# A free PSUM bank for the fill work, and attention values stored by chunks of 512 keys

## The chip, the core and the metric

The kernel runs on one core of a Trainium2 chip. The metric is the device time of one execution in microseconds (us). Five engines work side by side: PE (TensorE, matrix products), ACT (ScalarE), DVE (VectorE), POOL (GpSimd) and SP (SyncE, which here issues every DMA). They wait for each other on semaphores; each engine works its own list of instructions strictly in order.

## The reference

Two independent parts are computed from two inputs of 2048 tokens by 448 features, and their results stand side by side in the output.

```python
# part A: Fourier mixing, real part
a = einsum("bsd,ed->bse", x, dft_hid_re)
b = einsum("bsd,ed->bse", x, dft_hid_im)
y = einsum("ts,bse->bte", dft_seq_re, a) - einsum("ts,bse->bte", dft_seq_im, b)

# part B: full attention, 16 heads of 28
q, k, v = split(x @ wqkv)
p = softmax(einsum("bhqd,bhkd->bhqk", q, k) * 28 ** -0.5)
o = einsum("bhqk,bhkd->bhqd", p, v)
out_B = concat_heads(o) @ wo
```

## The kernel before

Each matrix operand is split into a high and a low part, and a product is the sum of several products of such parts.

**Attention.** A projection product (`project`, run through the helper `chain`, L571) makes queries and keys, transposed, in tiles of 128 rows by 512 tokens; the two parts go through SP to the DRAM tensor `qk_d` and come back per head as `q` and `k` tiles. `values` makes V token tile by token tile (16 tiles of 128 tokens, eleven products each). For each head, `head_once` walks over 16 key tiles times four chunks of 512 queries. `score` (L1130) multiplies one key tile with one query chunk into a PSUM bank, and ACT takes the exponential of that bank into a half of a `kept` buffer (L1134). After sixteen scores, `four` (L1141) multiplies the sixteen exponentials with V: this is called a **block** below, 64 blocks in all, four to a head. A block is one task on PE: it is not interrupted, and it waits until all of its sixteen exponentials are done. Its output is the bank `po`, held for the whole head. A column of ones beside the values of each head gives the sum of the exponentials; the rest of the 32 columns that a head takes are zeros. `tops` finds a bound for each query row out of the first 32 keys (the "key products", L1114); the `qb` tile that it loads has one buffer.

**The fill.** Everything else that PE does stands between the scores: the remaining projections, the hidden transform of part A (`hidden_both`, L571), the sequence transform with its halved matrices (`combine` prepares its operands on ACT and DVE, `sequence_halved` multiplies, L901; `middle`, L849), and the output projection (`project_late`, L1364 and L1395). ACT also splits the loaded weights (L542, L890), copies projections out of their banks (L612), shares the plain copies with DVE (L436 is ACT's, L438 DVE's), and splits the attention output for the last projection (L1349).

**The order.** The order of instructions on every engine is written by a planner at build time, `Schedule`. It walks through a model of the engines with a guessed duration for every task, and each time that an engine is free it takes the task with the smallest key that is ready and whose buffers can be had. The keys are due times: scores of head h get keys spread evenly from `T_ATT` to `T_END`, the fill (`fkey`) keys up to `T_FILL`, the end of the output projection keys from `T_OUT`. SP's DMAs are planned the same way, so a DMA that has to wait holds back all DMAs behind it.

**The banks.** PSUM has eight banks. Four belong to `fill_s` and four to `bank_s`, which serves scores, key products and block outputs. `bank_s` may borrow from `fill_s` (its `lender`): in `can_take`, L117, the free banks of both are added up. The `kept` pool has 19 buffers, each a pair of 128 by 512 tiles.

**The values.** For each token tile, `values` takes one `kept` pair and uses its first half: DVE copies the 448 columns out of the bank into runs of 28 (L639), sets the ones (L640) and the zeros (L641), and SP stores the tile to `v_d` (L643), whose rows hold, per head and partition, 16 token tiles of 32 numbers. One store thus writes 2,048 runs of 128 bytes. `head_loads` (L1010) loads a head's values once all sixteen stores have landed.

Of the kernel before, what the change touches and what calls it, by code (L numbers as in the profile page):

```python
# [21 lines left out]
D = 448  # L22
H = 16
DH = 28
# [5 lines left out]
VW = 32  # L30
# [5 lines left out]
NQS = 8  # L36
NQB = 1
NFILL = 4
NQ = 4
QT = NT // NQ  # L40
Q_YO = 2
# [57 lines left out]
class Slots:  # L99
# [17 lines left out]
    def can_take(self, slots, before):  # L117
        n = sum(since <= before for _, since in self.free)
        if self.lender:
            n += sum(since <= before for _, since in self.lender.free)  # L120
        if n < len(slots) + max(s.spare for s in slots):
            return False
        if self.in_turn:
            return all(s in self.turns[:n] for s in slots)
        return True
# [187 lines left out]
def tile_kernel(ctx, tc, xa, wre, wim, wd, xb, wqkv, wo, out):  # L313
    nc = tc.nc
# [15 lines left out]
    v_d = dram.tile([H, P, NT * VW], F32, name="vd")  # L330
# [6 lines left out]
    mid_d = dram.tile([1, D], F32, name="midd")  # L337
    far_d = [dram.tile([P, D], F32, name=f"fard{n}") for n in range(2 * NQ)]

# [13 lines left out]
    kept_s = new("kept", [P, 2, CH], F32, NPAIRS)  # L353
# [9 lines left out]
    ones = new("ones", [P, 1])  # L363
    diff = new("diff", [P, 2 * NQ + 1, 3 * QT + 1])
    whole = new("whole", [P, 2 * NQ + 1])
    alike = new("alike", [P, 2, 2 * NQ + 1])
    edge = new("edge", [P, 4, NT])
# [12 lines left out]
    sch.pools.append(raw_s)  # L380
    fill_s, bank_s = Slots(banks[:NFILL]), Slots(banks[NFILL:])
    bank_s.lender = fill_s
# [5 lines left out]
    nc.gpsimd.memset(diff[:, :, 3 * QT:], 0.0)  # L388
    nc.gpsimd.memset(diff[:, 2 * NQ, 4:3 * QT], 0.0)
    nc.vector.tensor_tensor(fold, ident[:, :VW], ident[:, VW:2 * VW], op=ALU.add)  # L390
# [19 lines left out]
    M512, M448, MS = 0.2335, 0.2050, 0.2365  # L410
# [3 lines left out]
    def pe(key, emit, n=1, d=MS, lat=0.25, **kw):  # L414
        return sch.add({"PE": n * d}, key, emit, lat=lat, **kw)

    def dma(key, emit, size=256, extra=0.0, n=1, **kw):

        return sch.add({"SP": 0.4}, key, lambda e: emit(), dmas=[(size, extra)] * n, **kw)
# [4 lines left out]
    def dve(key, emit, d=DVE_P, **kw):  # L424
        return sch.add({"DVE": d}, key, lambda e: emit(), **kw)

    def pool(key, emit, d, **kw):
        return sch.add({"POOL": d}, key, lambda e: emit(), **kw)
# [9 lines left out]
            nc.vector.tensor_copy(dst, src)  # L438


    T_ATT, T_END, T_FILL, T_OUT = 34.0, 755.0, 824.0, 766.0
    units = [(h, c) for h in range(H - 1) for c in range(NC)] + [(H - 1, c) for c in LAST]
    due, head_due, head_due_b = {}, {}, {}

# [120 lines left out]
    def chain(key, seq, o, cols, deps, use, d, then=(), parts=None, last=last):  # L565


        n = len(seq)
        for i, (w, x) in enumerate(seq):
            def emit(e, i=i, w=w, x=x):  # L570
                nc.tensor.matmul(o.t[:, :cols], w(), x(), start=(i == 0), stop=(i == n - 1))  # L571
            more = [*(deps if i == 0 else ()), *(parts.get(i, ()) if parts else ())]
            last[0] = pe(key + i * d, emit, d=d, deps=[last[0], *more], use=[*use, o, *(then if i == n - 1 else ())])
        return last[0]

    def lz(f, *a):
        return lambda: f(*a)
# [3 lines left out]
    v_done = {}  # L581
# [40 lines left out]
        return Piece(lambda: wqkv[:, :, j * P:(j + 1) * P], 0.2 if j == 0 else key, "w", j == 0)  # L622

    def values(ready, chunks):
        for c in chunks:
            v_done[c] = []
            for t in range(4):
                tok = slice(c * CH + t * P, c * CH + (t + 1) * P)
                o, pair = fill_s.slot(), kept_s.slot()
                vs = Half(pair, 0)  # L630
                seq = products(lambda k: lz(x_h, k, tok), lambda k: lz(x_l, k, tok), lambda: lz(x_3, tok),
                               lambda k: (lambda: w_first.h[:, k]), lambda k: (lambda: w_first.l[:, k]))
                key = fkey(11, M448)
                end = chain(key, seq, o, D, [], [], M448, [pair],
                            {3 * k: [xb_ready[c, k], ready[k], *ready[4:][:k // 3]] for k in range(4)}, v_last)

                def put(o=o, vs=vs):
                    v3 = vs.t.rearrange("p (h d) -> p h d", h=H)
                    nc.vector.tensor_copy(v3[:, :, :DH], o.t[:, :D].rearrange("p (h d) -> p h d", h=H))  # L639
                    nc.vector.memset(v3[:, :, DH:DH + 1], 1.0)  # L640
                    nc.vector.memset(v3[:, :, DH + 1:], 0.0)  # L641
                b = dve(key - 20, put, 0.85, deps=[end], use=[o, pair])
                v_done[c].append(dma(key - 20, lambda vs=vs, c=c, t=t: nc.sync.dma_start(  # L643
                    v_d[:, :, (4 * c + t) * VW:(4 * c + t + 1) * VW].rearrange("h p x -> p h x"),
                    vs.t.rearrange("p (h x) -> p h x", h=H)), extra=2.5, deps=[b], use=[pair]))


    y_stored = {}
# [374 lines left out]
    before = {}  # L1023
# [202 lines left out]
    o = bank_s.slot()  # L1226
# [18 lines left out]
    key = fkey(0, 0)  # L1245
# [175 lines left out]
    o = bank_s.slot()  # L1421
# [64 lines left out]
```

## Time and profile before

| | us |
|---|---|
| median of three timed runs | 865.23 (864.64 to 870.12) |
| profiled execution | 868.95 |
| its span, first to last instruction | 866.7 |
| mean granted clock of PE | 0.98 |
| PE, ACT, DVE, POOL busy | 843.5, 634.9, 375.6, 6.0 |
| first block starts | 83.4 |
| last block starts | 827.6 |

In the page's costliest groups a row names line, engine, operation, output and input tiles, shape and count; then busy us and the mean ns of one; then the idle time of the engine before them and what ended it. The chain of waits is followed back from the last instruction and lists start, length and what the time was spent on. In the tables by stretches each engine's busy time stands for a stretch of the span, then PE's granted clock, the share of DMA time and GB/s.

### The profile page before, as it was taken

What the parts mean: (1) busy time and instruction counts of PE and PEld (TensorE: products, weight loads), DVE (VectorE), ACT (ScalarE), POOL (GpSimd) and SP (SyncE); (2) the same over time, 40 slices, a digit from 0 to 9 for tenths busy, and PEclk for the clock granted to TensorE, in tenths of its full rate; (3) what the DMA queues carried; (4) which work ended last, traced back from release to release, by engine and by line L of the source; (5) the groups of instructions that cost most, each with busy time, mean ns of one, the idle gap of its engine ahead of it and who ended that gap; (6) DMA issues with size and microseconds to landing.
All of it is one profiled execution on the core that took longest, in us unless ns stands there. A gap on an engine that the chain in (4) does not pass through costs nothing.

```text
span 866.7 us, 14119 instructions
## 1 busy us (share of the span) xinstructions
PE 843.5 (97%) x4856; PEld 532.5 (61%) x4856; DVE 375.6 (43%) x888; ACT 634.9 (73%) x1287; POOL 6.0 (1%) x27
## 2 busy tenths in 40 slices
PE   8988999999999999999999999999999999999896
PEld 7875455556555556666556655667566656666575
DVE  7541013111311132222379463667766575756341
ACT  6107787787877878878899766789887876788831
POOL 2000000000000000000000000000000000000000
PEclk9998999999999999999989999999899999999999
DMA  9867634424343454434597664558886653746433
GB/s 285 207 113 192 193 116 123 158 90 133 100 152 111 127 155 122 132 112 142 172 219 220 204 189 137 179 171 246 192 250 208 191 171 119 224 144 175 125 117 106
DMA packets 156239, 141.27 MB, mean 163 GB/s; under 512 B 69310, under 2 KB 125120, under 8 KB 156160
## 3 DMA queue, kind: packets, MB, share of 16 engines
q1 hardware_dynamic: 156160, 140.29, 54.9%
q8 instruction: 40, 0.66, 0.3%
q14 instruction: 39, 0.32, 0.1%
HBM read 98.82 MB, written 43.12 MB: 164 GB/s over the span
## 4 chain that ended last, share of the span: by engine, by line
PE 86%; ACT 5%; DMA 4%; DVE 2%; SPq 1%; issue 1%; ACTq 0%; DVEq 0%
PE bank L1130 27%; PE bank L1141 25%; PE bank L571 18%; PE bank L901 10%; ACT kept L1134 3%; PE bank L1364 3%; DMA wraw<-wre 1%; PE bank L849 1%; DMA kept<-ond 1%; DMA qb<-qkd 1%; PE bank L1114 1%; DMA kept<-xb 1%; PE bank L1395 1%; DMA v<-vd 1%; PE bank L1221 1%
## 5 line engine op out<-in xcount | busy, mean ns | idle before, releaser
L1134 ACT ACTIVATE kept<-bank 128x512 f32<-128x512 f32 x1024 | 522.9, 669 | 104.6 <-PE bank L1130 103.6
L1130 PE MATMUL bank<-q,k 85*128 85x512 f32 x1024 | 345.4, 416 | 7.2 <-ACT kept L1134 3.7
L1130 PEld LDWEIGHTS bank<-q,k 85*128 85x128 f32 x1024 | 184.2, 190 | 104.9 <-ACT kept L1134 50.5
L1141 PE MATMUL bank<-kept,v 128*32 128x512 f32 x2048 | 236.3, 602 | 0.9 <-DMA v<-vd 0.9
L1141 PEld LDWEIGHTS bank<-kept,v 128*32 128x32 f32 x2048 | 60.6, 111 | 136.1 <-issue 131.4
L901 PE MATMUL bank<-big,wlo 128*128 128x226 f32 x512 | 96.9, 285 | 0.0
L901 PEld LDWEIGHTS bank<-big,wlo 128*128 128x128 f32 x512 | 85.7, 202 | 15.1 <-issue 7.5
L571 PE MATMUL bank<-big,whi 128*128 128x512 f32 (+1 forms) x260 | 93.3, 397 | 1.3 <-DVE big L432 1.0
L901 PE MATMUL bank<-big,whi 128*128 128x448 f32 (+1 forms) x256 | 74.7, 338 | 0.2 <-ACT kept L1134 0.2
L873 DVE TENSOR_REDUCE diff<-wlo 128x1 f32<-128x512 f32 x96 | 65.6, 683 | 2.5
L571 PEld LDWEIGHTS bank<-big,whi 128*128 128x128 f32 x260 | 48.5, 190 | 16.3 <-issue 2.8
L901 PEld LDWEIGHTS bank<-big,whi 128*128 128x128 f32 x256 | 50.9, 208 | 7.6 <-ACT kept L1134 2.2
L891 DVE TENSOR_TENSOR wlo<-wraw,whi 128x512 fp32r<-128x512 f32 x32 | 22.0, 688 | 62.9 <-PE bank L901 49.5
L613 DVE TENSOR_TENSOR wd<-bank,wd 128x512 fp32r<-128x512 f32 x16 | 11.1, 691 | 82.9 <-ACT wd L612 82.9
L571 PE MATMUL bank<-big,wlo 128*128 128x512 f32 x112 | 44.6, 400 | 0.0
L571 PE MATMUL bank<-wd,whi 128*128 128x450 f32 (+1 forms) x128 | 43.0, 376 | 0.0
L438 DVE COPY kept<-bank 128x450 f32<-128x450 f32 (+2 forms) x31 | 19.3, 622 | 54.4 <-PE bank L571 54.0
L546 DVE TENSOR_TENSOR wlo<-wraw,whi 128x384 fp32r<-128x384 f32 x23 | 12.8, 556 | 69.2 <-ACT whi L542 60.7
L612 ACT ACTIVATE wd<-bank 128x512 fp32r<-128x512 f32 x16 | 10.8, 676 | 42.2 <-PE bank L571 42.2
L571 PE MATMUL bank<-wd,big 128*128 128x448 f32 x176 | 38.3, 376 | 0.0
L571 PEld LDWEIGHTS bank<-wd,big 128*128 128x128 f32 x176 | 33.9, 194 | 3.9 <-issue 0.9
L1364 PE MATMUL bank<-big 128*128 128x448 f32 x144 | 33.0, 368 | 0.0
(117 smaller groups left out, 588.6 us busy)
## 6 DMA issues: line engine op xcount, KB each, us to landing
wdraw<-wre SPq DMA_DIRECT2D x48, 256.0 KB
wdraw<-wim SPq DMA_DIRECT2D x48, 256.0 KB
qkd<-wd SPq DMA_DIRECT2D x32, 256.0 KB
q<-qkd SPq DMA_DIRECT2D x64, 112.0 KB
k<-qkd SPq DMA_DIRECT2D x64, 112.0 KB
abd<-kept SPq DMA_DIRECT2D x16, 448.0 KB
kept<-abd SPq DMA_DIRECT2D x16, 448.0 KB
qkd<-kept SPq DMA_DIRECT2D x24, 256.0 KB
```

The source lines that it names most:

```text
L438: nc.vector.tensor_copy(dst, src)
L546: b = dve(at, lambda: nc.vector.tensor_tensor(self.lo.t[:, :n], raw.t[:, :n], f32(self.hi.t)[:, :n], op=ALU.subtract), 0.15 * n, deps=[a], ...
L571: nc.tensor.matmul(o.t[:, :cols], w(), x(), start=(i == 0), stop=(i == n - 1))
L612: a = act(key, lambda o=o, hi=hi: nc.scalar.activation(as_r(hi.t), o.t, AF.Copy), deps=[end], use=[o, *own])
L613: b = dve(key, lambda o=o, hi=hi, lo=lo: nc.vector.tensor_tensor(as_r(lo.t), o.t, as_f(hi.t), op=ALU.subtract), deps=[a], use=[o, *own])
L873: seen.append(dve(key, lambda: nc.vector.tensor_reduce(dst, f32(flat(src.t)), axis=AX.X, op=ALU.max, apply_absolute_value=True), 0.6, deps ...
L891: b = dve_on(key - 11.5, lambda e: e.tensor_tensor(turned(lo.t), read(same.t), f32(turned(hi.t)), op=ALU.subtract), 0.65, deps=[a], acq=[l ...
L901: nc.tensor.matmul(o.t[:, at0:at0 + n], cut_of(w.t, e, c), x(), start=first, stop=stop)
L1130: m = pe(key, lambda e: nc.tensor.matmul(b.t, KT[h][kt // 4].t[:KR + 1, kt % 4 * P:(kt % 4 + 1) * P], q.t[:KR + 1, :], start=True, stop=True),
L1134: return act(key - 20, lambda: nc.scalar.activation(p.t, b.t, AF.Exp, scale=SCALE), deps=[m], use=[b, pair])
L1141: nc.tensor.matmul(o.t[j * VW:(j + 1) * VW, :], VT[h].t[:, kt // 4, kt % 4, :], tiles[i // 2].t[:, i % 2, :], start=(kt < 4 // len(cs)), s ...
L1364: nc.tensor.matmul(o.t[:, :D], a(), b(), start=(i == 0), stop=(i == 8 and n < N_HELD))
```

## The change

Three things are changed.

1. In `can_take`, scores (and all that draws on `bank_s`) may borrow all of the fill's free banks but one (`LEFT = 1`).
2. The planner's four due times move: attention from 28 to 723 instead of 34 to 755, the fill to 850 instead of 824, the last projection from 801 instead of 766.
3. `values` works on a chunk of 512 keys at a time. Two `kept` pairs hold the chunk, one for each eight heads, laid out so that the four token tiles of a head lie side by side. For each token tile DVE copies 8 heads into each pair, two copies instead of one. The ones and zeros of a pair are set once by POOL, in four memsets, with a key that lets them run early. SP then stores a pair with 1,024 runs of 512 bytes. There are eight stores instead of sixteen, and 32 memsets on POOL instead of 32 on DVE.

```diff
+LEFT = 1
...
         if self.lender:
-            n += sum(since <= before for _, since in self.lender.free)
+            n += max(0, sum(since <= before for _, since in self.lender.free) - LEFT)
...
-    T_ATT, T_END, T_FILL, T_OUT = 34.0, 755.0, 824.0, 766.0
+    T_ATT, T_END, T_FILL, T_OUT = 28.0, 723.0, 850.0, 801.0
...
     def values(ready, chunks):
+        HH = H // 2
         for c in chunks:
-            v_done[c] = []
+            v_done[c], puts = [], [[], []]
+            pairs = [kept_s.slot() for _ in range(2)]
+            heads = lambda pair: pair.t.rearrange("p a (b t x) -> p (a b) t x", t=4, x=VW)
             for t in range(4):
                 tok = slice(c * CH + t * P, c * CH + (t + 1) * P)
-                o, pair = fill_s.slot(), kept_s.slot()
-                vs = Half(pair, 0)
+                o = fill_s.slot()
...
-                end = chain(key, seq, o, D, [], [], M448, [pair],
+                end = chain(key, seq, o, D, [], [], M448, pairs,
...
-                def put(o=o, vs=vs):
-                    v3 = vs.t.rearrange("p (h d) -> p h d", h=H)
-                    nc.vector.tensor_copy(v3[:, :, :DH], o.t[:, :D].rearrange("p (h d) -> p h d", h=H))
-                    nc.vector.memset(v3[:, :, DH:DH + 1], 1.0)
-                    nc.vector.memset(v3[:, :, DH + 1:], 0.0)
-                b = dve(key - 20, put, 0.85, deps=[end], use=[o, pair])
-                v_done[c].append(dma(key - 20, lambda vs=vs, c=c, t=t: nc.sync.dma_start(
-                    v_d[:, :, (4 * c + t) * VW:(4 * c + t + 1) * VW].rearrange("h p x -> p h x"),
-                    vs.t.rearrange("p (h x) -> p h x", h=H)), extra=2.5, deps=[b], use=[pair]))
+                for i, pair in enumerate(pairs):
+                    if t == 0:
+                        def rest(pair=pair):
+                            blocks = pair.t.rearrange("p a (b x) -> p a b x", x=VW)
+                            for a in range(2):
+                                nc.gpsimd.memset(blocks[:, a, :, DH:DH + 1], 1.0)
+                                nc.gpsimd.memset(blocks[:, a, :, DH + 1:], 0.0)
+                        puts[i].append(pool(key - 25, rest, 1.2, use=[pair]))
+                    puts[i].append(dve(key - 20, lambda o=o, i=i, pair=pair, t=t: nc.vector.tensor_copy(
+                        heads(pair)[:, :, t, :DH], o.t[:, i * HH * DH:(i + 1) * HH * DH].rearrange("p (h d) -> p h d", h=HH)), 0.35,
+                        deps=[end], use=[o, pair]))
+            for i, pair in enumerate(pairs):
+                v_done[c].append(dma(key - 20, lambda i=i, pair=pair, c=c: nc.sync.dma_start(
+                    v_d[i * HH:(i + 1) * HH, :, 4 * c * VW:4 * (c + 1) * VW].rearrange("h p x -> p h x"),
+                    pair.t.rearrange("p a (b x) -> p (a b) x", x=4 * VW)), 512, extra=1.0, deps=puts[i], use=[pair]))
```

Bank numbers and due times reach the program only through the planner, so the order of the instructions shows what they do. The first place is PE's list around block 2, before the change: the last product of block 1, the scores (L1130) of the following blocks, the first product of block 2 (L1141). Banks 0 to 3 are the fill's.

```order
L1141 MATMUL bank1_271<-kept16_251,v0_223 32x512 x2
L1130 MATMUL bank5_275<-q1_226,k1_219 128x512
L1130 MATMUL bank6_276<-q2_227,k1_219 128x512
L1130 MATMUL bank7_277<-q3_228,k1_219 128x512
L1130 MATMUL bank4_274<-q0_225,k2_220 128x512
L1130 MATMUL bank2_272<-q1_226,k2_220 128x512
L1130 MATMUL bank5_275<-q2_227,k2_220 128x512
L1130 MATMUL bank3_273<-q3_228,k2_220 128x512
L1130 MATMUL bank6_276<-q0_225,k2_220 128x512
L1130 MATMUL bank0_270<-q1_226,k2_220 128x512
L1141 MATMUL bank1_271<-kept17_252,v0_223 32x512 x2
```

The same place after the change, up to the middle of what stands between blocks 1 and 2 (the lines are eight higher, L1138 the scores, L1149 the blocks, L572 the projections).

```order
L1149 MATMUL bank5_275<-kept1_236,v0_223 32x512 x2
L1138 MATMUL bank6_276<-q0_225,k1_219 128x512
L1138 MATMUL bank7_277<-q1_226,k1_219 128x512
L1138 MATMUL bank4_274<-q2_227,k1_219 128x512
L1138 MATMUL bank2_272<-q3_228,k1_219 128x512
L1138 MATMUL bank0_270<-q0_225,k1_219 128x512
L572 MATMUL bank1_271<-big_206,whi2_213 128x512
L1138 MATMUL bank6_276<-q1_226,k1_219 128x512
L572 MATMUL bank1_271<-big_206,wlo2_216 128x512
L1138 MATMUL bank7_277<-q2_227,k1_219 128x512
L572 MATMUL bank1_271<-big_206,whi2_213 128x512
L1138 MATMUL bank4_274<-q3_228,k1_219 128x512
```

Before, scores and the block output stand in all four of the fill's banks, and no fill stands between the blocks. Now a projection keeps a bank and advances by one product after nearly every score.

The second place is ACT's list near the end of the attention, before the change: L1349 splits the attention output, here the part that the second load brings; L1134 are exponentials, L436 is a copy.

```order
L1134 ACTIVATE kept_239<-bank_274 128x512
L1134 ACTIVATE kept_243<-bank_275 128x512
L1349 ACTIVATE big<-kept_248 128x512 x2
L1349 ACTIVATE big<-kept_237 128x512
L1349 ACTIVATE big<-kept_253 128x512
L1349 ACTIVATE big<-kept_237 128x512
L1349 ACTIVATE big<-kept_253 128x512
L436 ACTIVATE kept_241<-bank_277 128x512
L1134 ACTIVATE kept_243<-bank_276 128x512
L1134 ACTIVATE kept_244<-bank_274 128x512
```

The same place after (L1142 the exponentials, L1357 the splits, L1392 those of the last rows).

```order
L1142 ACTIVATE kept_237<-bank_271 128x512
L1142 ACTIVATE kept_243<-bank_277 128x512
L1142 ACTIVATE kept_243<-bank_275 128x512
L1357 ACTIVATE big<-kept_239 128x512
L1392 ACTIVATE q_225<-kept_252 128x512
L1357 ACTIVATE big<-kept_248 128x512 x2
L437 ACTIVATE kept_247<-bank_276 128x512
L1357 ACTIVATE big<-kept_246 128x512
L1357 ACTIVATE big<-kept_249 128x512
```

The six splits that follow the second load stood ahead of the last exponentials; now they stand behind them.

## The prediction

> **What bounds the kernel now.** I began with the page's busy times and costliest groups (busy us, mean ns of one, then idle before).
>
> ```profile
> PE 843.5 (97%) x4856; PEld 532.5 (61%) x4856; DVE 375.6 (43%) x888; ACT 634.9 (73%) x1287; POOL 6.0 (1%) x27
> ...
> L1134 ACT ACTIVATE kept<-bank 128x512 f32<-128x512 f32 x1024 | 522.9, 669 | 104.6 <-PE bank L1130 103.6
> L1130 PE MATMUL bank<-q,k 85*128 85x512 f32 x1024 | 345.4, 416 | 7.2 <-ACT kept L1134 3.7
> ```
>
> PE looks full, but its busy time is modelled: a matmul's mean here is 416 ns although scores follow each other far closer. So I counted by stretches of the span (PE, PEld, DVE, ACT, POOL busy; clock; DMA share; GB/s).
>
> ```profile
> 84.00:91.00 7.00, 7.00 (x39) 2.46 (x31) 0.69 (x1) 2.52 (x7) 0.00 (x0) 0.68 0.67 203
> 91.00:110.00 19.00, 19.00 (x100) 7.69 (x98) 0.75 (x2) 16.83 (x36) 0.00 (x0) 1.00 0.60 182
> 110.00:424.00 314.00, 313.87 (x1761) 185.86 (x1764) 70.24 (x141) 250.29 (x504) 0.61 (x2) 1.00 0.41 129
> ...
> 436.00:452.00 16.00, 15.96 (x77) 9.78 (x73) 11.64 (x32) 15.04 (x37) 0.00 (x0) 0.79 0.90 215
> ...
> 787.00:831.00 44.00, 41.77 (x239) 22.91 (x231) 19.25 (x39) 34.30 (x71) 0.00 (x0) 0.96 0.40 121
> ```
>
> From 110 to 424 ACT is idle for 64 us of 314. The waits of the stretch 91 to 424 (total, times, longest) say where, and the timeline of one block (start, length) says why.
>
> ```profile
> ACT kept L1134 <- PE bank L1130: 47.8, 45, 3.2
> ...
> PEld bank L1130 <- ACT kept L1134: 23.9, 103, 0.5
> ```
>
> ```profile
> 203.69 3.64 PE L1141 MATMUL bank<-kept,v 128*32 128x512 f32 x32
> ...
> 207.26 0.73 PE L571 MATMUL bank<-big,whi 128*128 128x512 f32 x2
> ...
> 208.76 0.40 PE L1130 MATMUL bank<-q,k 85*128 85x512 f32 x1
> ...
> 209.20 0.60 ACT L1134 ACTIVATE kept<-bank 128x512 f32<-128x512 f32 x1 [1.09 <-PE bank L1130]
> ```
>
> A block of sixteen PV products holds PE for 3.57 us (203.69 to 207.26). It starts only when its sixteen exponentials are done, and while it runs no score can follow, so ACT lives on the scores already standing in banks. It then runs dry until the next score plus a hand-over of 0.44 us (208.76 to 209.20). Between two such gaps ACT is nearly always busy. So the period of a block is set on ACT: 16 × 0.511 (522.9 / 1024) = 8.2 us of exponentials, plus whatever else ACT does, plus a dry time of 3.57 + 0.44 − 0.511 × (scores ahead). PE fills the rest with projection and Fourier products, and scores wait for ACT. The chain of waits confirms it at the start, where PE had no such products:
>
> ```profile
> 10.29 23.43 PE bank L571 x108
> ...
> 35.23 9.21 PE bank L571 x45
> ...
> 51.34 2.92 DMA qb<-qkd
> ...
> 78.08 5.14 DMA v<-vd
> 83.36 6.17 PE bank L1141 x32
> ...
> 91.86 3.57 PE bank L1141 x32
> ...
> 101.03 3.57 PE bank L1141 x32
> ...
> 110.20 3.57 PE bank L1141 x32
> ...
> 423.65 3.57 PE bank L1141 x32
> ...
> 707.41 3.80 DMA qb<-qkd
> ...
> 808.78 7.42 DMA kept<-ond
> ...
> 827.64 3.57 PE bank L1141 x32
> ...
> 846.77 10.88 PE bank L1364 x54
> ```
>
> Blocks 2 to 4 are 9.17 us apart with six scores ahead; the formula gives 8.2 + 4.0 − 3.1 = 9.1. Blocks 4 to 31 are 11.6 apart, blocks 31 to 64 about 12.2.
>
> **The change part by part.** The sum is made against the profiled execution, 868.95 us with a span of 866.7; it lies 0.4% above the median of the timed runs, 865.23, so I carry the difference over to the median.
>
> *Value stores.* Sixteen stores of 128-byte runs become eight of 512-byte runs. The DMA view of 45 to 50 us, nearly all value stores, and of 22 to 24 us, mostly 512-byte pieces of the weights, give the price (packets, MB, share of 16 engines):
>
> ```profile
> q1 hardware_dynamic: 5613, 0.71, 89.9%
> q1 hardware_dynamic: 615, 0.30, 69.0%
> ```
>
> The first is 0.899 × 16 × 5 / 5613 = 12.8 ns a packet, the second at most 36 ns. 32,768 packets at 12.8 ns over 16 engines are 26 us; 8,192 at 36 ns are 18 us, an upper bound. What counts for the end, though, is which wait goes with it:
>
> ```profile
> 42.80 5.32 SPq L643 DMA_DIRECT2D vd<-kept  x4
> L643 SPq DMA_DIRECT2D vd<-kept x16: 382/591/2790, 16.0 to 70.2; - x16
> ```
>
> Before the first PV block the chain waits 2.9 us for a load of qb, which stood in SP's queue behind four value stores, and 5.1 us for v, which needs all sixteen, the last issued at 70.2. In the new order the first block stands behind 111 projection, 176 value, 20 score and 4 key products. By rows, a value product is 9.21 / 45 = 0.205 us and a projection (23.43 − 64 × 0.205) / 44 = 0.235, a score of the same 512 columns likewise: 10.3 + 26.1 + 36.0 + 4.7 + 1.6 = 78.7 us, the key products at an estimated 0.4 each, under two scores' price. The last value store can be issued near 60 and the v load near 65, landing at 70: hidden with 8 us to spare. So block 1 starts at 78.7 instead of 83.4: **−4.7**. If the cover goes, nothing is gained there.
>
> *Edits I cost at nothing.* The new value copies (32 for 16, on DVE) and the memsets that leave DVE:
>
> ```profile
> 14.22 0.61 DVE L639 COPY kept<-bank 128x448 f32<-128x448 f32 x1
> 14.80 0.07 DVE L640 MEMSET kept<- 128x16 f32 x1
> 1.42 0.10 POOL L389 MEMSET diff<- 128x8 f32 x1
> 4.00 0.21 POOL L396 MEMSET kb<- 128x128 f32 x1
> ```
>
> A half copy lies between 0.31 and 0.61 us, so a token tile costs DVE 0.6 to 1.2 us while PE works 11 × 0.205 = 2.3 us on it. The 32 memsets on POOL are 3 to 7 us at 0.10 to 0.21; twelve of them now stand ahead of the zeros of the first projection weights, which thus come at 4.2 + 12 × 0.2 = 6.6, and PE starts at 10.3. The value buffers hold eight of nineteen kept pairs, so the last x loads wait for buffers in SP's queue; what they bring is first needed at 10.3 + 44 × 0.205 + 33 × 0.235 = 27 us, and the other eleven buffers turn over long before.
>
> *The bank left to the fill.* Four groups of ACT's other work set the prices of this part and the next:
>
> ```profile
> L612 ACT ACTIVATE kept<-bank 128x512 fp32r<-128x512 f32 x12 | 8.0, 670 | 3.7 <-PE bank L571 2.0 <-issue 1.3 <-PE bank L1130 0.4
> L436 ACT ACTIVATE kept<-bank 128x446 f32<-128x446 f32 (+3 forms) x23 | 13.4, 585 | 13.3 <-PE bank L1141 6.0 <-PE bank L1364 4.2 <-PE bank L571 3.0
> L542 ACT ACTIVATE whi<-wraw 128x512 fp32r<-128x512 f32 x23 | 16.8, 740 | 1.7 <-DMA wraw<-wqkv 1.7
> L1349 ACT ACTIVATE big<-kept 128x512 fp32r<-128x512 f32 x12 | 6.9, 627 | 2.3 <-DMA kept<-ond 2.3
> ```
>
> In the old order nothing but scores stands between blocks 1 and 4; now 12 to 14 projection products stand in each gap. These three periods become, with 3.7 scores ahead and 1.2 copies of a projection (L612) on ACT, 8.2 + 2.1 + 0.8 = 11.1 us instead of 8.9: **+6.5**. Block 4 then starts at 112.0, 1.8 us later than before, but with 62 more projection products and 3 fewer scores done: 13.9 us of PE work in hand. Whether that lead is worth anything depends on ACT.
>
> *What ACT is spared later.* Between blocks 5 and 64 the new order has 15 projection copies on ACT for 20, 8 copies of hidden and output rows for 20 (the others moved to DVE or past the end), 5 splits of the attention output for 12, one weight split fewer. 5 × 0.670 + 12 × 0.585 + 7 × 0.627 + 0.740 = 15.5 us by means; in a run they overlap as exponentials do (511 of 669), 11.8. I take **−14**.
>
> *Fewer scores ahead.* The price of the free bank: counted in the order, the scores ahead of a block fall from 4.15 to 3.56 (27 blocks) and from 3.12 to 2.56 (33 blocks), 0.30 and 0.29 us more dry time each. Against that, the fill between a block and its first score falls from 0.31 to 0.04 and from 0.20 to 0.02 us. Net 27 × 0.03 + 33 × 0.11 = **+4.4**.
>
> *The end.* 124 instead of 98 output products stand behind block 64: 26 × 10.88 / 54 = **+5.2**. In exchange the wait at 808.8 should go. It is ACT's: a split of the attention output (L1349) waits there for its load, and exponentials are queued behind it on ACT, scores behind these on PE, which from 787 to 831 is 2.2 us unbusy and loses 44 × 0.04 = 1.8 to the clock. In the new order the splits of that second load stand behind the last exponential: **−4**. The qb wait at 707 stays.
>
> Sum: −4.7 + 6.5 − 14 + 4.4 + 5.2 − 4 = −6.6 us: 862.3 for such an execution, **858.6** on the median's scale.
>
> **The rivals.**
> *PE sets the pace.* Then the 13.9 us in hand are kept, less the 1.8: 865.2 − 12.1 − 4 = 849. For it: scores wait only 23.9 us for ACT in 333. Against: ACT's gaps, which fit the formula. 0.25.
>
> *The start stays.* The v load stands behind stores of projections in SP's queue whatever the values do; if block 1 stays at 83.4 and the wait at the end finds a successor: 858.6 + 4.7 + 4 = 867, no change. 0.17.
>
> *ACT starves (slower).* Where the fill holds three banks and one stays free, scores have three. If the dry time grows by 0.30 a block but the fill ahead of the first score was hidden anyway (ACT still had work), 27 × 0.27 + 33 × 0.18 = 13.2 us are not won back; with ACT's lower price (2.2) and another wait at the end (4) that gives 878. It decides from a dry time of some 2.3 us a block on, against 47.8 / 28 = 1.7 now. 0.13.
>
> *The clock.* More short pauses on PE could halve its clock, as in 84 to 91 (0.68) and 436 to 452 (0.79). The loss is 7 × 0.32 = 2.2 and 16 × 0.21 = 3.4 us there; six such stretches more, at 2.8 on average, are +17: 876. The Trainium skill (TensorE: Matmul & The Clock Gate, A second HAM failure mode: psum-queue depth-cycling) tells of just that, pauses between groups of matmuls that cycle through banks. By that rule the time is 876, by the rows 858.6. The trace speaks against: in 91 to 110 scores come at ACT's pace in seven banks, and the clock is 1.00. 0.05.
>
> **How the numbers follow.** My case has 0.40; its own range is 852 to 865. About 1% (856.6 to 873.9) is what a measurement of this kernel can tell from no change. Faster: 0.16 of my case, 0.24 of the PE rival, 0.02 of the start: 0.42. Slower: 0.12 of the starved ACT, 0.05 of the clock, 0.03 of the rest: 0.20. Same: 0.38. The range reaches down past 849 by the scores' other waits and up to within 4 us of the slow cases: 842 to 874.
>
> **What would show it.** Block 1 near 79 and a v load landed by 71 (else the start rival); projection products between blocks 1 and 4, and block 4 near 112; blocks 5 to 31 about 11.3 apart, with ACT's wait for scores per block still near 1.7 (2.3 or more: starved; periods near 10.8: PE's pace); PE after the last block longer by 5 us; no wait for ond before it. The forecast is wrong if the period does not follow ACT's work, or if new DMA waits appear in the Fourier stage.

## The result and the profile after

The changed kernel takes **828.01 us** (median of four runs, 826.59 to 829.16) against 867.67 for the kernel before on the same chip: a ratio of **0.9526, 95% interval 0.945 to 0.9602**. The forecast was 858.6 with a range of 842 to 874, so the direction was right and the size far off: 40 us instead of 7. The profiled execution took 829.04, its span 827.2.

The page of the kernel after, busy times and the group of the exponentials (lines eight higher than before):

```profile
PE 814.4 (98%) x4856; PEld 531.0 (64%) x4856; DVE 383.2 (46%) x882; ACT 622.9 (75%) x1277; POOL 8.3 (1%) x59
...
L1142 ACT ACTIVATE kept<-bank 128x512 f32<-128x512 f32 x1024 | 511.1, 677 | 118.8 <-PE bank L1138 118.4
```

The same 1024 exponentials: 522.9 us busy and 104.6 us of waits before, 511.1 and 118.8 now. By this row ACT waits longer for scores, yet the kernel is 40 us faster. The row counts only the idle time directly ahead of an exponential; all of ACT's idle time fell from 231.8 us (span 866.7 less 634.9 busy) to 204.3. So the row doesn't tell the story. The chain of waits after:

```profile
57.53 12.56 PE bank L572 x53
...
77.14 3.57 PE bank L1149 x32
...
108.70 3.57 PE bank L1149 x32
...
397.87 3.57 PE bank L1149 x32
...
420.10 5.41 DMA wdraw<-wre
...
783.41 3.57 PE bank L1149 x32
...
807.77 10.88 PE bank L1372 x54
```

Behind the first load of `xb`, which stands at the head of both chains, no DMA is left before the first block, and the waits for `qb` near 707 and for `ond` near 809 are gone. Loads of the operands of the second Fourier stage stand in both chains; the first is that of `wdraw` shown here.

I cut both spans at the starts of blocks 1, 4, 31 and 64 as the trace has them: 83.36, 110.13, 423.58 and 827.57 before; 77.06, 108.63, 397.80 and 783.34 after. Before, in the table by stretches (PE, PEld, DVE, ACT, POOL busy; clock; DMA share; GB/s):

```profile
83.36:110.13 26.77, 26.77 (x137) 10.34 (x137) 1.45 (x3) 20.12 (x42) 0.00 (x0) 0.90 0.62 190
110.13:423.58 313.45, 313.32 (x1757) 185.70 (x1756) 70.24 (x141) 249.74 (x503) 0.61 (x2) 1.00 0.41 128
423.58:827.57 403.99, 397.08 (x2479) 250.56 (x2479) 253.79 (x619) 324.60 (x674) 0.47 (x1) 0.97 0.63 185
```

After:

```profile
77.06:108.63 31.57, 31.57 (x183) 18.10 (x182) 3.99 (x8) 26.81 (x56) 0.61 (x2) 1.00 0.57 173
108.63:397.80 289.17, 289.17 (x1688) 174.84 (x1687) 71.02 (x142) 237.38 (x486) 0.00 (x0) 1.00 0.39 126
397.80:783.34 385.54, 381.88 (x2464) 245.52 (x2463) 251.19 (x611) 317.25 (x666) 0.47 (x1) 0.99 0.64 192
```

| us | before | after | change |
|---|---|---|---|
| start of block 1 | 83.36 | 77.06 | −6.3 |
| blocks 1 to 4 | 26.77 | 31.57 | +4.8 |
| blocks 4 to 31: ACT busy | 249.7 | 237.4 | −12.4 |
| blocks 4 to 31: ACT idle | 63.7 | 51.8 | −11.9 |
| blocks 31 to 64: ACT busy | 324.6 | 317.3 | −7.4 |
| blocks 31 to 64: ACT idle | 79.4 | 68.3 | −11.1 |
| start of block 64 to the end | 39.1 | 43.8 | +4.7 |
| sum | 866.7 | 827.2 | −39.5 |

The ends came about as forecast. The gain lies in the sixty block periods between them: 11.61 us each became 10.71, and 12.24 became 11.68; about half of that is time in which ACT was idle. Two things happened in these periods. They hold 88 fill products fewer (fill is here every product on PE but scores and blocks, as the trace counts them): 23 of these now stand before block 1, 39 between blocks 1 and 4, 26 behind the start of block 64. And what is left in them waits less. The waits of blocks 4 to 31 show where (total, times, longest). Before:

```profile
ACT kept L1134 <- PE bank L1130: 45.6, 43, 3.2
PEld bank L1130 <- ACT kept L1134: 18.8, 84, 0.5
```

After:

```profile
ACT kept L1142 <- PE bank L1138: 38.9, 19, 2.8
PEld bank L1138 <- ACT kept L1142: 5.9, 30, 0.3
```

ACT waits for a score 19 times instead of 43 in 27 blocks, and the scores' wait for ACT has shrunk to a third. ACT's list through two such periods shows what happened. Before (blocks start at 215.5, 226.9 and 238.0; start, length, and in brackets the idle time ahead):

```profile
219.72 4.17 ACT L1134 ACTIVATE kept<-bank 128x512 f32<-128x512 f32 x8
223.76 0.61 ACT L612 ACTIVATE kept<-bank 128x512 fp32r<-128x512 f32 x1
224.26 4.53 ACT L1134 ACTIVATE kept<-bank 128x512 f32<-128x512 f32 x9
231.13 0.60 ACT L1134 ACTIVATE kept<-bank 128x512 f32<-128x512 f32 x1 [2.34 <-PE bank L1130]
232.07 0.60 ACT L1134 ACTIVATE kept<-bank 128x512 f32<-128x512 f32 x1 [0.34 <-PE bank L1130]
233.00 5.50 ACT L1134 ACTIVATE kept<-bank 128x512 f32<-128x512 f32 x11 [0.33 <-PE bank L1130]
238.26 0.72 ACT L612 ACTIVATE kept<-bank 128x512 fp32r<-128x512 f32 x1
```

After (blocks start at 215.9, 226.7 and 237.7):

```profile
216.74 0.78 ACT L613 ACTIVATE kept<-bank 128x512 fp32r<-128x512 f32 x1
219.88 7.95 ACT L1142 ACTIVATE kept<-bank 128x512 f32<-128x512 f32 x16 [2.37 <-PE bank L1138]
227.53 0.79 ACT L613 ACTIVATE kept<-bank 128x512 fp32r<-128x512 f32 x1
230.69 7.94 ACT L1142 ACTIVATE kept<-bank 128x512 f32<-128x512 f32 x16 [2.38 <-PE bank L1138]
```

Before, a copy of a projection (223.76) cuts the exponentials in two, and where three fill products stand between two scores ACT waits 0.3 us for each (232.07, 233.00). After, the exponentials run in one piece of sixteen, 0.48 us apart, and the copy stands at the head of the dry time (the wait for the first new score behind a block), which it fills. In blocks 4 to 31 three fill products stand in a row between scores 75 times before and 20 times after, a single one 37 and 232 times; the runs of exponentials are broken 78 times before and 27 times after, which is once a period. I cut every period in the same way, in us, from the trace's records. The third row is the kernel after without the free bank, a run told of below:

| | period | fill products in it | block start to first exponential of a new score | from there to the next block: exponentials, other work, idle |
|---|---|---|---|---|
| blocks 4 to 31, before | 11.61 | 17.1 | 4.45 | 6.45 + 0.32 + 0.40 |
| after | 10.71 | 14.5 | 4.21 | 6.50 + 0.00 + 0.00 |
| after, no free bank | 11.70 | 15.0 | 4.55 | 6.05 + 0.47 + 0.63 |
| blocks 31 to 64, before | 12.24 | 27.2 | 4.63 | 6.96 + 0.36 + 0.30 |
| after | 11.68 | 26.7 | 4.42 | 7.01 + 0.17 + 0.08 |

So in blocks 4 to 31 the change took the other work and the small waits out of the run of exponentials (0.72 us a block) and brought the first score closer to the block (0.24). An obvious rival is that the periods are shorter only because they hold less fill: 2.6 products of some 0.2 us are 0.5 us. The third row speaks against it. With nearly as little fill (15.0) and everything else as in the kernel after, the period stays at 11.70; putting the free bank in takes 0.99 off it, of which the half product less explains 0.1. But the fill that went elsewhere is what lets PE follow the shorter period: at 0.235 us for a score and for a fill product of 512 columns, PE's work in a period of the kernel after is up to 3.57 + 30.5 × 0.235 = 10.7 us, nearly all of it. One experiment (the planner told of the doubled exponential) had one disturbed execution, the profiled one, which is not read; its ratio is worked out without it.

### The profile page after: what moved, and what is told of

Same layout as the page of the kernel before. It is cut to its first block, busy times and chain, and to the rows that moved or that the text cites. A ratio compares the mean times of both kernels' runs of the same rounds, so it can differ in the third digit from the quotient of the medians.

```text
span 827.2 us, 14140 instructions
## 1 busy us (share of the span) xinstructions
PE 814.4 (98%) x4856; PEld 531.0 (64%) x4856; DVE 383.2 (46%) x882; ACT 622.9 (75%) x1277; POOL 8.3 (1%) x59
## 4 chain that ended last, share of the span: by engine, by line
PE 88%; ACT 5%; DMA 4%; DVE 1%; issue 1%; SPq 0%; ACTq 0%; DVEq 0%
PE bank L1138 28%; PE bank L1149 25%; PE bank L572 19%; PE bank L909 9%; PE bank L1372 4%; ACT kept L1142 3%; DMA wdraw<-wre 2%; PE bank L857 1%; PE bank L1122 1%; DMA wraw<-wre 1%; ACT big L797 1%; PE bank L1403 1%; DMA kept<-xb 1%; ACT big L792 1%; PE bank L1229 0%
## 5 line engine op out<-in xcount | busy, mean ns | idle before, releaser
L1142 ACT ACTIVATE kept<-bank 128x512 f32<-128x512 f32 x1024 | 511.1, 677 | 118.8 <-PE bank L1138 118.4
L1138 PE MATMUL bank<-q,k 85*128 85x512 f32 x1024 | 371.0, 409 | 1.6 <-DVE kept L1125 0.9
L1138 PEld LDWEIGHTS bank<-q,k 85*128 85x128 f32 x1024 | 186.4, 189 | 98.3 <-issue 42.0
L1149 PE MATMUL bank<-kept,v 128*32 128x512 f32 x2048 | 237.6, 605 | 0.0
L1149 PEld LDWEIGHTS bank<-kept,v 128*32 128x32 f32 x2048 | 60.8, 111 | 134.9 <-issue 127.6
L909 PE MATMUL bank<-big,wlo 128*128 128x226 f32 x512 | 104.4, 277 | 1.0 <-DVE wlo L899 1.0
L909 PEld LDWEIGHTS bank<-big,wlo 128*128 128x128 f32 x512 | 95.7, 198 | 9.8 <-DVE wlo L899 1.3
L572 PE MATMUL bank<-big,whi 128*128 128x512 f32 (+1 forms) x260 | 96.6, 392 | 0.9 <-ACT big L511 0.7
L439 DVE COPY kept<-bank 128x450 f32<-128x450 f32 (+2 forms) x43 | 26.7, 620 | 81.7 <-PE bank L572 71.1
L572 PEld LDWEIGHTS bank<-big,whi 128*128 128x128 f32 x260 | 49.3, 191 | 9.7 <-ACT big L511 1.1
L572 PE MATMUL bank<-big,wlo 128*128 128x512 f32 x112 | 44.2, 396 | 0.0
L572 PE MATMUL bank<-wd,whi 128*128 128x450 f32 (+1 forms) x128 | 41.6, 368 | 0.0
L572 PE MATMUL bank<-wd,big 128*128 128x448 f32 x176 | 37.6, 370 | 0.0
L572 PEld LDWEIGHTS bank<-wd,big 128*128 128x128 f32 x176 | 32.9, 188 | 3.9 <-issue 0.7
L1202 ACT ACTIVATE kept<-bank 128x512 f32<-128x512 f32 (+1 forms) x19 | 11.6, 610 | 25.6 <-PE bank L1149 25.5
L928 DVE TENSOR_TENSOR wlo<-wdraw,wraw 128x256 fp32r<-128x256 f32 x64 | 24.3, 420 | 14.0 <-PE bank L909 13.3
```

The source lines that it names most:

```text
L909: nc.tensor.matmul(o.t[:, at0:at0 + n], cut_of(w.t, e, c), x(), start=first, stop=stop)
L928: e.tensor_tensor(turned(dl.t, c, 2, HP), read(r.t, c, 2, HP), read(base.t, c, 2, HP), op=op)
L1138: m = pe(key, lambda e: nc.tensor.matmul(b.t, KT[h][kt // 4].t[:KR + 1, kt % 4 * P:(kt % 4 + 1) * P], q.t[:KR + 1, :], start=True, stop=True),
L1142: return act(key - 20, lambda: nc.scalar.activation(p.t, b.t, AF.Exp, scale=SCALE), deps=[m], use=[b, pair])
L1149: nc.tensor.matmul(o.t[j * VW:(j + 1) * VW, :], VT[h].t[:, kt // 4, kt % 4, :], tiles[i // 2].t[:, i % 2, :], start=(kt < 4 // len(cs)), s ...
L1202: a = act(key - 20, lambda: nc.scalar.activation(osb.t[:n * VW], o.t[:n * VW], AF.Copy, accum_out=sums[:n * VW, g:g + 1]), deps=[dep], use ...
```

## The experiments

At first I held that PE's work had become the pace (theory A below); the third group of runs showed that this is half of the account.

### Each part alone

The free bank alone (kernel before, every line as it was but the one in `can_take` and its constant):

```diff
+LEFT = 1
-            n += sum(since <= before for _, since in self.lender.free)
+            n += max(0, sum(since <= before for _, since in self.lender.free) - LEFT)
```

> The kernel before with the free bank alone (LEFT = 1), old due times, old value stores. Theory A (the free bank lets one fill product stand behind every score, so that PE and ACT work at the same time instead of by turns, and PE's own work becomes the pace): most of the gain comes with this line, about 833 us, blocks 5 to 31 near 10.8 apart. Theory B (the due times: the lead of the attention over the fill makes the gain): about 860. Theory C (the value stores and the earlier start): about 865.

Measured 844.37, ratio 0.9734 (0.968 to 0.9788): 23 of the 40 us, less than theory A's 833 had it. Blocks 4 to 31 are 11.01 apart, with 15.9 fill products in each, and 31 to 64 12.05.

The due times alone:

```diff
-    T_ATT, T_END, T_FILL, T_OUT = 34.0, 755.0, 824.0, 766.0
+    T_ATT, T_END, T_FILL, T_OUT = 28.0, 723.0, 850.0, 801.0
```

> The kernel before with the new due times alone; scores may still borrow every bank. Theory A: no gain, 863 to 870, blocks 5 to 31 near 11.5 apart. Theory B: most of the gain, about 835. Theory C: about 866.

Measured 879.82, 1.0167 (1.01 to 1.0233): slower. Blocks 4 to 31 stay 11.70 apart, and 62.3 us instead of 39.1 lie behind the start of block 64, since 233 fill products are left there, against 134.

The value stores alone (the third part of the diff alone):

> The kernel before with the new value stores alone. Theories A and B: only the start moves, block 1 some 4 to 6 us earlier, and the time by as much or less: 860 to 865. Theory C: 845 or less.

Measured 870.98, 1.0042 (1.0001 to 1.0083). Block 1 starts 1.1 us earlier, at 82.28, with 22 more fill products ahead of it, and nothing comes of it at the end.

The kernel after without the free bank:

```diff
-LEFT = 1
+LEFT = 0
```

> The kernel after without the free bank (LEFT = 0): new due times and new value stores stay. Theory A: nearly all of the gain goes, 855 to 863, blocks 5 to 31 near 11.5 apart. Theory B: about 833. Theory C: about 845.

Measured 882.68, 1.0203 (1.0137 to 1.0269). Block 1 starts at 77.94, near the 77.06 of the kernel after, and the kernel is slower than before. So everything hangs on the free bank: without it the two other parts, alone or together, gain nothing. Against the kernel after, 26.7 us are lost in blocks 4 to 31 and 19.1 behind the start of block 64, where 233 fill products are left instead of 160. With the free bank, the count of runs of eight or more scores in a row in PE's order falls from 25 to 2 in blocks 4 to 31 (6 with the free bank alone, 23 without it).

### The parts in pairs

The free bank and the due times, old stores:

> The kernel before with the free bank and the new due times, old value stores. Reckoned in PE's idle time with the clock's loss, by the runs so far: the free bank takes 12 us out of blocks 2 to 31 and 6 out of the later blocks, the due times 8 out of the later blocks, but they put back 9 behind the last block where much fill is left for it (here 225 products of the output, as with the due times alone): about 844, no gain over the free bank alone. If instead the due times are worth in this company what the kernel after shows over the free bank (16 us) whatever the stores do: about 829.

Measured 854.39, 0.9888 (0.9848 to 0.9928): 10 us worse than the free bank alone, and worse than both expectations. Blocks 4 to 31 reach the 10.71 of the kernel after, but 298 instead of 313 fill products stand ahead of block 1, and in the second Fourier stage two blocks, 50 and 51, have no fill at all by the order. The row of that stretch:

```profile
620.00:645.00 25.00, 24.01 (x105) 9.98 (x104) 12.80 (x33) 23.92 (x53) 0.00 (x0) 0.80 0.62 158
```

ACT is full there (it makes the Fourier operands as well), PE waits, and its clock is 0.80. The end, 60.1 us from the start of block 64, is as long as without the free bank.

The free bank and the value stores, old due times:

> The kernel before with the free bank and the new value stores, old due times. By the same reckoning: 844 with the free bank alone, less about 8 for the start (the stores and the later start of block 1 with more fill ahead of it): about 836; block 1 near 80, blocks 5 to 31 near 10.7 apart, the later blocks as with the free bank alone (12.0). If the due times alone are what joins with the free bank: 844.

Measured 842.51, 0.9771 (0.9723 to 0.9819). Blocks 4 to 31 are 10.69 apart, later ones 12.06. So the value stores add nothing to the free bank alone (0.9734), and a good deal once the due times are new too: from 0.9888, the pair above, to the 0.9526 of all three. Between the profiles of these two, block 1 starts 8 us earlier, blocks 31 to 64 take 9 us less and the end 16 us less. The stores reach the end only through the order that the planner makes with them; why that order leaves 160 fill products there instead of 228 stays open.

Only the attention's due times (28 to 723) new, the fill's and the last projection's old, with free bank and stores:

> The kernel after with only the attention's due times moved (28 to 723); the fill's and the last projection's stay at 824 and 766 as before. With all due times old it took 842.5. If the attention's times make what the new due times bring: 826 to 830. If the fill's later times make it: about 840.

Measured 828.07, 0.9553 (0.9499 to 0.9606), as the kernel after. The kernel after again, on the same chip:

> The kernel after once more, on the same chip as the three others, so that a few us can be compared: 0.945 to 0.960 of the kernel before.

Measured 827.16, 0.9544 (0.9485 to 0.9602). So of the new due times only the attention's matter. They act in blocks 31 to 64: 398.0 us with the old ones, 383.2 with the new. There the gain is mostly in single long periods: those above 12.6 us exceed the median period by 17.2 us in sum with the old times, by 5.5 with the new (19.6 in the kernel before). Two executions of the kernel after itself differ here by 4 us (9.6 and 5.6). The ones followed in the traces are blocks at which the fill runs short or waits for operands or loads. Why the earlier attention meets fewer of them, I could not read off the order; that stays open.

Other times for the fill, as a possible better version:

```diff
-    T_ATT, T_END, T_FILL, T_OUT = 28.0, 723.0, 850.0, 801.0
+    T_ATT, T_END, T_FILL, T_OUT = 28.0, 723.0, 835.0, 785.0
```

> The kernel after with the fill's due time at 835 instead of 850 and the last projection's at 785 instead of 801 (before: 824 and 766). In the order no block between the first and the last is left with fewer than 12 fill products (in the kernel after one has 9, block 34, with 0.5 of the clock). If it is such blocks that still cost (two blocks took 28.4 us there instead of 23): 4 to 6 us less than the kernel after, about 823. If the wait there is that of the operands of the second Fourier stage, whatever the order: no change, 826 to 830.

Measured 828.81, 0.9565 (0.9523 to 0.9607): no change. The period of block 34 fell from 14.5 us (13.0 in the second profile of the kernel after) to under 12.6, and those of 48 and 53 rose to 13.1 and 12.9 instead.

### Who sets the period

Two banks left to the fill (`LEFT = 2` in the kernel after):

> The kernel after with two banks left to the fill instead of one. In blocks 5 to 31 the scores ahead of a block fall from 3.6 to 2.7 by the order, 0.42 us more dry time on ACT a block. If ACT sets the period (the prediction's theory): 27 x 0.42 = 11 us more, about 839, blocks 5 to 31 further apart by 0.4 than PE's work in them explains. If PE's own work sets it (theory A): the period follows the fill put into it (two products more a block, 0.45 us, which come off the end), PE's idle stays near 0.25 a block, and the time stays at 825 to 832.

Measured 841.32, 0.9743 (0.9696 to 0.979): the total that the prediction's theory gave, but not for its reason. Blocks 4 to 28 are 11.18 apart against 10.71, 0.47 more where 0.42 was expected from ACT's dry time. But 16.8 instead of 14.4 fill products stand in each, and 2.4 × 0.2 us of PE's work are 0.5 as well, so these periods do not tell the theories apart. Theory A missed the total chiefly because three longer periods follow (13.1, 14.0, 11.9), where the order holds too little fill; the clock of 395 to 419 is 0.86.

One exponential of each sixteen computed twice, the first (kernel after):

```diff
-        return act(key - 20, lambda: nc.scalar.activation(p.t, b.t, AF.Exp, scale=SCALE), deps=[m], use=[b, pair])
+        def exp():
+            for _ in range(2 if kt % 4 == 0 and c == 0 else 1):
+                nc.scalar.activation(p.t, b.t, AF.Exp, scale=SCALE)
+        return act(key - 20, exp, deps=[m], use=[b, pair])
```

> The kernel after, in which one exponential of every sixteen is computed twice (the same result in the same place): 64 more on ACT, 0.51 us each a block. If ACT sets the period: 64 x 0.51 = 33 us more, about 861. If PE sets it: much of it is taken up by ACT's idle time, a quarter to a half comes through (ACT's waits around the blocks): 835 to 845.

The same in the kernel before:

> The kernel before, with the same addition: one exponential of every sixteen computed twice, 0.51 us of ACT a block, 33 us in all. If ACT sets the period of the kernel before (the prediction's theory): 33 us more, about 897. If PE and ACT work by turns there (long stretches of scores alone at ACT's pace, then fill alone at PE's): what falls into the stretches of scores alone comes through, the rest does not; more than in the kernel after, 8 to 20 us: 873 to 885.

Measured 832.60, 0.965 (0.9603 to 0.9698), and 874.29, 1.0046 (1.0011 to 1.0082). Of the 64 × 0.48 = 31 us put in, some 5 come through in either kernel (some 10 in the kernel after, if one goes by the ratios). That looked like the end of the prediction's theory, but the first exponential is one of the scores ahead: its second run falls into the dry time, and ACT's theory would forgive it too. My expectation had overlooked that. The same with the ninth exponential (`kt % 4 == 2`), in the kernel after and in the kernel before:

> The kernel after, with the ninth exponential of every sixteen computed twice instead of the first. The first one's second run falls where the scores ahead of a block are worked off, into the time in which ACT is dry anyway, so that a period set on ACT would not have grown by it: those two runs did not tell the theories apart. The ninth is never among the scores ahead (3.6 and 2.6 on the mean). If ACT sets the period: 64 x 0.51 = 33 us more, about 861. If PE's work sets it and ACT's lateness is met by fill: under 10 us more, 829 to 838.

> The kernel before, with the ninth exponential of every sixteen computed twice. If ACT sets the period there (the prediction): 33 us more, about 900. If it does so only in the stretches of scores alone: 8 to 20 us more, 875 to 887. In either case more comes through than in the kernel after.

Measured 864.68, 1.0004 (0.9976 to 1.0031), and 894.38, 1.0301 (1.0239 to 1.0363): 37 us more than the kernel after and 29 more than the kernel before on the same chip, where 31 were put in. The same work costs little in one place and all of its time in the other. The stretches of blocks 4 to 31, first exponential and then ninth, in the kernel after:

```profile
109.27:398.51 289.24, 289.24 (x1688) 175.34 (x1687) 70.96 (x142) 253.38 (x512) 0.00 (x0) 1.00 0.39 126
```

```profile
111.38:416.70 305.32, 298.98 (x1689) 169.53 (x1688) 71.17 (x142) 253.46 (x512) 0.00 (x0) 1.00 0.37 119
```

ACT is equally busy, 253.4 us, and the stretch is 16 us longer, with the same 14.5 fill products in a period. One period of each: with either doubled, the run of seventeen takes 8.57 us instead of 7.95. With the first one doubled the wait ahead of it falls from 2.4 to 1.7 us; with the ninth it stays.

```profile
218.47 0.62 ACT L613 ACTIVATE kept<-bank 128x512 fp32r<-128x512 f32 x1
220.83 8.57 ACT L1144 ACTIVATE kept<-bank 128x512 f32<-128x512 f32 x17 [1.74 <-PE bank L1138]
```

```profile
225.56 0.72 ACT L613 ACTIVATE kept<-bank 128x512 fp32r<-128x512 f32 x1
228.67 8.57 ACT L1144 ACTIVATE kept<-bank 128x512 f32<-128x512 f32 x17 [2.38 <-PE bank L1138]
```

So a period is a circuit: a block, a score, its exponential, the run of exponentials up to the last that the next block needs. What stands in that run counts in full, what stands in the dry time counts little.

Does the order matter, or ACT alone? The ninth exponential doubled with the planner told of it:

```diff
+        return act(key - 20, exp, 2 * ACT_P if kt % 4 == 2 and c == 0 else ACT_P, deps=[m], use=[b, pair])
```

> The kernel after with the ninth exponential of every sixteen computed twice, as in the run that took 864.7, but the planner is told: it reckons 0.96 us instead of 0.48 for these 64. ACT's work is the same as there. The planner now puts 16.3 fill products into a block of the first stage where it put 14.2, and 102 instead of 157 stand behind the last block. If a circuit through ACT is the limit whatever the order: blocks 5 to 31 stay 11.3 apart and the 55 products (0.2 us each) that leave the end are all that comes back, 853. If what costs is that the order reckons with too little time on ACT, so that PE waits at a fixed place: PE's idle time in blocks 5 to 31 falls from 0.85 to about 0.3 a block, and 835 to 848 is left.

Measured 859.60, 0.9962 (0.9926 to 0.9998), against 1.0004 where the planner did not know: 0.4% back, nearer to the 853 of the circuit than to the other case. An order that knows of the longer run hardly helps against it.

Two scores of each sixteen computed twice, in the kernel after and in the kernel before:

```diff
+        def mm(e):
+            for _ in range(2 if kt % 4 in (0, 2) and c == 0 else 1):
+                nc.tensor.matmul(b.t, KT[h][kt // 4].t[:KR + 1, kt % 4 * P:(kt % 4 + 1) * P], q.t[:KR + 1, :], start=True, stop=True)
```

> The kernel after, in which two scores of every sixteen are computed twice (the same product into the same bank): 128 products of 512 columns more on PE, 0.235 us each, 30 us in all. If PE's own work is the pace: nearly all of it comes through, 26 to 31 us, about 856. If ACT sets the period: PE has time to spare where scores wait for ACT, and 0 to 10 us come through.

> The kernel before with the same two scores of every sixteen computed twice, 30 us of PE. By turns (theory A): in the stretches of scores alone PE waits for ACT and has room for them, elsewhere not: 15 to 26 us come through, less than in the kernel after. If ACT sets the period: 0 to 10 us.

Measured 850.17, 0.9804 (0.9767 to 0.984), and 880.25, 1.0147 (1.01 to 1.0193): 22 of 30 us come through after, 11 before, both between what the two theories expected. Blocks 4 to 31 are 11.12 apart (10.71 plus 0.41 of the 0.47 put in) after, 11.85 (11.61 plus 0.24) before. PE had room for half of it before, and nearly none now. So in the kernel after PE's work and ACT's run both set the period: theory A was half right, and the prediction's the other half.

An exponential reckoned at 0.50 us instead of 0.48 in the planner (`ACT_P`, kernel after), as a possible better version:

> The kernel after with 0.50 us instead of 0.48 for an exponential in the planner (measured in the kernel before: 0.511). In the order 15.0 instead of 14.2 fill products stand in a block of the first stage, 145 instead of 157 behind the last block, and two blocks of the second Fourier stage have none. If the balance of PE and ACT in the kernel after can still be bettered: 820 to 826. If PE's idle time in an ordinary block (0.25 us) is all that can be had and the two blocks cost 3 to 5 us each: 828 to 836.

Measured 834.42, 0.9637 (0.9608 to 0.9665): worse. Blocks 4 to 31 are 10.85 apart, with 15.3 fill products in each instead of 14.5. None of the versions tried beats the kernel after.

## Why the prediction was wrong

By its own steps:

- *Block 1 starts 78.7 instead of 83.4* (−4.7): right in kind, measured −6.3. The value loads are hidden, as it said. Their rows and, for 54.4 to 60 us, the DMA's (packets, MB, share):

```profile
L1018 SPq DMA_DIRECT2D v<-vd x16: 319/367/589, 66.3 to 697.6; - x16
L651 SPq DMA_DIRECT2D vd<-kept x8: 377/490/622, 20.8 to 58.9; - x8
```

```profile
q1 hardware_dynamic: 2309, 1.35, 84.7%
```

  The last store is issued at 58.9, the first load at 66.3, eleven us ahead of block 1. A packet costs 0.847 × 16 × 5.6 / 2309 = 33 ns, under the bound of 36. But an earlier start alone is worth nothing (871 with the stores alone).
- *Three periods of blocks 1–4 11.1 instead of 8.9* (+6.5): measured 10.5, +4.8.
- *The period of a block is set on ACT*: right in both kernels, as the doubled ninth exponential shows, but not alone: of 30 us more work on PE 11 came through before and 22 after.
- *Fewer scores ahead* (+4.4): **here the sum failed.** The step let ACT's idle time grow by 4.4 us where it fell by 23.0. Its two terms came as priced: in blocks 4 to 31 0.33 us of exponentials less stood ahead (0.30 forecast), and the first new score came 0.24 us sooner (0.27). It rests on the sentence "Between two such gaps ACT is nearly always busy", which I read off totals: of the 63.7 us idle in blocks 4 to 31, 0.40 × 27 = 11 lay between the gaps, in short waits such as the 0.3 us above (43 waits in 27 blocks was the sign, in the row that I quoted as 45 in 47.8 us); in blocks 31 to 64 it was 0.30 × 33 = 10. The even order took most of them away, 18 us in sum, for which the prediction had no term, although the order rows ahead of it show a fill product after nearly every score.
- *What ACT is spared* (−14): measured −19.8 of ACT's busy time. The 25 instructions fewer are there as counted, but they make only some 8 us of it; some 12 are exponentials, which overlap more in unbroken runs and which no step had. And what counts for the period is where the rest stands: in blocks 4 to 31 other work of ACT in the run of exponentials fell from 0.32 to 0.00 us a block, in the dry time it rose from 0.72 to 0.85. The formula added "whatever else ACT does" in full, and should have added only what stands in the run.
- *The end* (+5.2 and −4): measured +4.7; the long block 63 (16.3 us) is gone. *The qb wait at 707 stays*: wrong, the period of block 54 fell from 15.5 to 12.8.
- Blocks 31 to 64: +3.6 for the scores ahead, −4 for the wait near their end and a part of the −14 were forecast, −18.5 measured. Some 10 of these are long periods (eight above 12.6 us became four); apart from block 63's no step had them, and they hang on the attention's due times. The rows' clock is 0.97 before and 0.99 after; its share was not separated.

The rivals: *PE sets the pace* (849) came nearer, and PE is full now, but it priced only the lead at the start, not the shorter run on ACT. *ACT starves* fell: ACT's idle time became shorter, not longer. *The start stays* fell with block 1 at 77.06. *The clock*: granted 1.00 from 108.6 to 397.8, where scores and fill alternate between banks. The Trainium skill (TensorE: Matmul & The Clock Gate, A second HAM failure mode: psum-queue depth-cycling) tells of clock lost where the matmuls cycle through banks with small idle times between their groups; no such loss shows in this stretch. A lack of fill does not settle the clock either: it was 0.80 in the row of blocks 50 and 51 above, but 1.00 from 91 to 110 before, also without fill. The 0.90 over blocks 1 to 4 before comes from 84 to 91 (0.68), just behind the wait for `v`.

## What to carry to other kernels

Where an engine waits for a batch of another's results, write the period down as a circuit and ask of each piece of work whether it stands on the circuit or beside it; the same instruction, 64 times, cost some 5 or 37 us here by its place. Idle time in many short waits is worth as much as in a few long ones, and a count of waits per period shows it where their total does not. A buffer kept free for low-priority work can speed up the high-priority work, because it lets the two alternate evenly instead of by turns. And before a shorter period is read as a faster one, count the work that was moved out of it, and find a run that moves the work without the change.

## What the runs showed of the chip

An exponential of 128 by 512 lasts 0.60 us by itself and follows the one before it after 0.48 (sixteen in 7.95 us); each break in a run thus costs 0.12 us besides the wait. By that, the 51 breaks fewer in blocks 4 to 31 are 6 us of the 7.6 by which the exponentials there got shorter. PE's clock stayed at 1.00 for the 289 us in which scores and fill alternate; what lowered it elsewhere was not tested.
